# An instruction counter in the planner of a fused attention and feed-forward kernel, and a new instruction order under it

## Chip, cores, metric

One core of one Trainium2 chip. The metric is device time in microseconds (us) of that core, the median of the fast runs. A profile's span, from the first to the last instruction, is some 1.7 us shorter than the time of the same run.

## The reference, cut to what matters

Two branches read the same input (2048 x 512, bf16): A, an attention of 32 heads of 16 in 4 segments of 512 positions with a memory carried from segment to segment, and B, a gated feed-forward of width 1792. A gate mixes them.

```python
for s in range(4):                        # A
    p = softmax(qs @ ks.T * scale + mask)
    a_dot = p @ vs
    a_mem = (phi(qs) @ M) / (phi(qs) @ z + 1e-6)
    outs.append(g * a_mem + (1 - g) * a_dot)
    M = M + phi(ks).T @ vs                # the "memory burst" below
    z = z + phi(ks).sum()
a = concat(outs) @ wo
gate = x @ W_gate; up = x @ W_up          # B
b = (relu(gate) * up) @ W_down
out = sigmoid(x . gate_w) * a + (1 - ...) * b
```

## The kernel before: what the argument touches

The kernel's code contains a planner. Every piece of work is an `Op` with a planned duration on each engine that may run it. `Sched.run` simulates the engines, always taking the piece with the lowest key among those that can start soonest, and the resulting order is what is emitted. `NUDGE` holds shifts of keys that a search found. The plan fixes only the order on each engine; on the chip an instruction may still wait, as a matmul of experiment 3 did for its weights, 2.02 us.

```python
if e == "PE":
    o.ran = mode if mode in o.flex else o.mode   # tile shape: D, R, P or C
    if o.ran != mode:
        dur += SW                                # 0.094 for a change of shape
        mode = o.ran
```

TensorE's matmuls have four tile shapes here (in brackets as the profile's rows give them): D, the full array (`128*128`); R, row tiles for score blocks (`32*128`); P, for attention times V (`64*32`); C, column tiles for the memory burst (`128*32`), in which full-array work may ride along as four instructions in place of one:

```python
def mm(out_ap, lhsT, rhs, start, stop):
    if tiling[0] == "C":
        for j in range(4):
            q = slice(32 * j, 32 * j + 32)
            nc.tensor.matmul(out_ap[q], lhsT=lhsT[:, q], rhs=rhs, ..., tile_position=(0, 32 * j))   # cut
    else:
        nc.tensor.matmul(out_ap, lhsT=lhsT, rhs=rhs, start=start, stop=stop)

def mz_mm(s, g):                                 # memory burst: 64 matmuls of 34 columns, 0.56 us
    for c in range(NC):
        for t in range(4):
            for j in range(4):
                h = 8 * c + 2 * j
                nc.tensor.matmul(...)            # cut
```

Attention times V is 64 matmuls planned at 1.015 us. Each matmul has a weight load of its own (the trace of before has 1024 of each for the 16 blocks of attention times V, 192 of each for the three memory bursts), so both are bursts of 128 instructions. The program opens with warm-up matmuls that compute nothing:

```python
for _ in range(31):
    nc.tensor.matmul(g_dummy.t[:, 0:P], lhsT=ones, rhs=ones, start=True, stop=True)
```

The softmax here doesn't subtract the row's maximum and nothing guards it: scores larger than these inputs give would overflow.

## Time and profile before

| | before |
|---|---|
| time | 267.15 us (266.64 to 267.41, 6 runs) |
| span of the profiled run | 265.0 us |
| TensorE busy | 256.7 us, 97% |
| longest idle time of TensorE | 1.14 us at 34.9 us, "issue" |
| changes of tile shape on TensorE | 161 |

The profile's lines are shown in the prediction. Its key habit: TensorE's busy share doesn't say whether it is full, because the profile models the ends of matmuls. Starts are what count, and weight loads, of which the trace has 2886 where it has 2853 matmuls, number the instructions: load number n is taken as instruction 2n.

### The profile page before, as it was taken

To read this page: it belongs to the slowest core of one execution; us is meant where nothing else is said; L and a number is where in the kernel's file an instruction comes from. 1 tells how busy PE (TensorE), PEld (TensorE's weight loads), DVE (VectorE), ACT (ScalarE), POOL (GpSimd) and SP (SyncE) were. 2 spreads that over 40 slices of the span, in tenths; PEclk is the share of its full clock that TensorE was granted. 3 is DMA by queue.
4 is the path that set the end of the run, shared out by engine and by line. 5 is a ranking of instruction groups with operands and counts; after the bars stand their busy time and mean duration, and the time that the engine had idled before them with its cause. 6 is when DMAs were issued, how large, how long until landed. Compare 5 with 4: busy or idle time off the path is not lost.

```text
span 265.0 us, 7147 instructions
## 1 busy us (share of the span) xinstructions
PE 256.7 (97%) x2853; PEld 116.7 (44%) x2886; DVE 183.6 (69%) x413; ACT 193.4 (73%) x187; POOL 175.2 (66%) x436
## 2 busy tenths in 40 slices
PE   8999989999999999999999999999999999999995
PEld 7443433444444443434453444444444344344454
DVE  1488878878858675787889678786987036848352
ACT  3598978988787678989787569777878656778201
POOL 8326768886878887466599878764778746665400
PEclk9999999999999999999999999999999999999999
DMA  5998296222435010001821010000021001000002
GB/s 161 294 238 194 64 332 106 91 71 82 109 92 115 22 41 22 20 2 40 161 50 49 20 43 1 2 1 22 0 56 40 0 24 41 22 0 2 2 0 79
DMA packets 27761, 17.96 MB, mean 68 GB/s; under 512 B 14032, under 2 KB 27088, under 8 KB 27728
## 3 DMA queue, kind: packets, MB, share of 16 engines
q1 hardware_dynamic: 27136, 16.72, 25.1%
q0 software_dynamic: 176, 0.52, 0.6%
q8 instruction: 22, 0.36, 0.6%
q10 hardware_dynamic: 416, 0.26, 0.3%
q14 instruction: 11, 0.09, 0.1%
HBM read 9.84 MB, written 2.10 MB: 45 GB/s over the span
## 4 chain that ended last, share of the span: by engine, by line
PE 92%; issue 3%; ACT 2%; DMA 2%; DVE 0%; ACTq 0%
PE G L264 71%; PE S L774 9%; PE G L886 7%; PE G L262 3%; DMA wk_sb<-in_A_wk_dram 2%; PE G L306 1%; PE G L647 1%; ACT E L788 1%; ACT Vp L556 0%; PE G L823 0%; ACT QT L556 0%; ACT etq L579 0%; DVE xT L429 0%; ACT os L695 0%; PE G L421 0%
## 5 line engine op out<-in xcount | busy, mean ns | idle before, releaser
L788 ACT ACTIVATE E<-S 128x2048 bf16<-128x2048 f32 x72 | 135.1, 1876 | 35.7 <-PE S L774 30.8
L798 POOL TENSOR_SCALAR_AFFINE_SELECT E<-E 64x256 bf16<-64x256 bf16 x256 | 116.1, 454 | 61.9 <-ACT E L788 48.1
L264 PE MATMUL G<-xT,wg_sb 128*128 128x512 bf16 x200 | 53.9, 380 | 0.6 <-issue 0.3
L264 PE MATMUL G<-wd_sb,hT 128*128 128x512 bf16 (+2 forms) x239 | 53.1, 354 | 1.4 <-issue 1.1
L264 PE MATMUL G<-xT,wu_sb 128*128 128x512 bf16 x196 | 53.0, 380 | 0.2
L699 DVE TENSOR_TENSOR hT<-G,os 128x512 bf16<-128x512 f32 x56 | 38.4, 686 | 19.3 <-PE G L264 12.0
L921 DVE STREAM_TRANSPOSE T<-G 128x512 f32<-128x512 f32 x44 | 29.9, 700 | 16.0 <-PE G L886 14.3
L695 ACT ACTIVATE os<-G 128x512 bf16<-128x512 f32 x56 | 33.2, 596 | 5.6 <-PE G L264 5.2
L264 PEld LDWEIGHTS <-hT 128*128 128x128 bf16 x252 | 22.2, 98 | 24.0 <-issue 2.4
L264 PEld LDWEIGHTS <-wg_sb 128*128 128x128 bf16 x208 | 18.9, 98 | 23.2 <-issue 2.5
L264 PEld LDWEIGHTS <-wu_sb 128*128 128x128 bf16 x202 | 18.7, 98 | 23.3 <-issue 2.8
L774 PE MATMUL S<-QT,K 32*128 32x192 bf16 (+7 forms) x512 | 28.6, 287 | 0.3
L735 DVE TENSOR_SCALAR os<-G,ngcol 128x512 bf16<-128x512 f32 (+2 forms) x13 | 8.7, 669 | 19.5 <-PE G L264 19.4
L774 PEld LDWEIGHTS <-K 32*128 32x128 bf16 x512 | 8.2, 92 | 30.2 <-issue 30.1
L886 PE MATMUL G<-E,Vp 64*32 64x128 bf16 (+7 forms) x512 | 19.0, 284 | 1.1 <-issue 1.1
L886 PE MATMUL G<-E,VS 64*32 64x128 bf16 (+7 forms) x512 | 18.5, 284 | 0.0
L264 PE MATMUL G<-wo_sb,oT 128*128 128x512 bf16 (+2 forms) x71 | 16.9, 355 | 0.2 <-issue 0.2
L518 POOL COPY R<-rcol 32x4 f32<-32x4 f32 x64 | 14.2, 222 | 2.9
L264 PE MATMUL G<-xT,wk_sb 128*128 128x512 bf16 x61 | 15.8, 380 | 0.2
L886 PEld LDWEIGHTS <-Vp 64*32 64x32 bf16 x512 | 12.2, 91 | 7.3 <-issue 4.9
L941 DVE TENSOR_TENSOR O<-T,sm 128x256 bf16<-128x256 f32 x32 | 14.9, 498 | 0.2
L264 PE MATMUL G<-wv_sb,xT 128*128 128x512 bf16 x62 | 14.9, 380 | 0.1
(95 smaller groups left out, 278.7 us busy)
## 6 DMA issues: line engine op xcount, KB each, us to landing
VS<-Vp SPq DMA_DIRECT2D x8, 296.0 KB, 3.6
out_dram<-os SPq DMA_DIRECT2D x15, 128.0 KB, 1.7
xn<-in_A_x_dram SPq DMA_DIRECT2D x3, 512.0 KB, 5.0
wd_sb<-in_B_W_down_dram SPq DMA_DIRECT2D x3, 512.0 KB, 3.6
wg_sb<-in_B_W_gate_dram SPq DMA_DIRECT2D x2, 512.0 KB, 6.2
wu_sb<-in_B_W_up_dram SPq DMA_DIRECT2D x2, 512.0 KB, 6.9
wg_sb<-in_B_W_gate_dram SPq DMA_DIRECT2D x3, 256.0 KB, 6.1
wu_sb<-in_B_W_up_dram SPq DMA_DIRECT2D x3, 256.0 KB, 6.4
```

Of the source, the lines that this page charges most:

```text
L262: nc.tensor.matmul(out_ap[q], lhsT=lhsT[:, q], rhs=rhs, start=start, stop=stop, tile_position=(0, 32 * j))
L264: nc.tensor.matmul(out_ap, lhsT=lhsT, rhs=rhs, start=start, stop=stop)
L518: nc.gpsimd.tensor_copy(R[s][32 * j:32 * j + 32, k, :], rcol[32 * k:32 * k + 32, cols])
L695: nc.scalar.activation(rg.t[:], g.t[:], ACT.Relu)
L699: nc.vector.tensor_tensor(h.t[:], u.t[:], rg.t[:], ALU.mult)
L735: nc.vector.tensor_scalar(ob.t[:, cs], g.t[:, 0:W], ngcol[:, tt:tt + 1], None, ALU.mult)
L774: nc.tensor.matmul(sp.t[:, j, off:off + w], lhsT=K2[s, cc].t[rows, kb, :, :].rearrange("p r k -> p (r k)"), rhs=QT[s, cc].t[rows, L - w:L] ...
L788: nc.scalar.activation(eb_.t[:], sp.t[:], ACT.Exp, scale=SCALE)
L798: nc.gpsimd.affine_select(out=v, in_=v, compare_op=ALU.is_ge, fill=0.0, base=0, pattern=[[0, 4], [1, 64]], channel_multiplier=-1)
L886: nc.tensor.matmul(gs[r].t[32 * j:32 * j + 32, L - w:L], lhsT=v, rhs=src.t[rows, j, off:off + w], start=(kb == 0), stop=(kb == 7), tile_po ...
L921: nc.vector.transpose(T.t[:].rearrange("p b e -> p (b e)"), g.t[:])
L941: nc.vector.tensor_tensor(O.t[:, :, r, :], T.t[:, :, 0:DH], sm.t[:, r, :, None].to_broadcast([P, 16, DH]), ALU.mult)
```

## The change

The intent: if TensorE's instructions are brought to it in pieces of 256 ("lines" from here on), a burst that uses up 256 in less time than fetching takes would stop. The planner gets a counter of instructions for each operation and lets none start earlier than 4.0 us after the planned start of the operation that holds the instruction 256 before its own last one (the code takes the end of the operation ahead of that one). A new search under that rule gave 86 shifts.

```diff
+FETCH, REFILL = 256, 4.0
 NUDGE = {
-    "d130.0": 50, "q21/0": 52, ...     (cut)
+    "g2.5/0": 24, "d300.0": 88, ...    (cut: 86 entries)
 }
+        o.count = count or 2 * max(1, round(engs.get("PE", 0) / MM))
...
+                    if e == "PE":
+                        k = issued[-1] + o.count * (4 if mode == "C" and "C" in o.flex else 1) - FETCH
+                        if k > 0:
+                            t = max(t, begun[bisect.bisect_left(issued, k) - 1] + REFILL)
...
+            if e == "PE":
+                begun.append(o.end)
+                issued.append(issued[-1] + o.count * (4 if o.ran == "C" and "C" in o.flex else 1))
...
-        a = op(f"pv{s}{c}", {"PE": 1.015}, ..., mode="P", alloc=gs, ...)             (cut)
+        a = op(f"pv{s}{c}", {"PE": 1.015}, ..., mode="P", count=128, alloc=gs, ...)  (cut)
```

The counts of the other bursts (memory 128, score blocks 8 for each part, denominators 8) are set likewise.

## The prediction

> **What bounds the kernel now.** I read the page first, then TensorE's waits, then the one stretch in which TensorE waits, then the DMA view of that stretch.

> From the page, busy time of TensorE, the granted clock, and the queue that carries instructions:

> ```profile
> PE 256.7 (97%) x2853; PEld 116.7 (44%) x2886; DVE 183.6 (69%) x413; ACT 193.4 (73%) x187; POOL 175.2 (66%) x436
> ...
> PEclk9999999999999999999999999999999999999999
> ...
> q8 instruction: 22, 0.36, 0.6%
> ```

> TensorE is the bound: 97% of 265.0 us at full clock, the next engine at 73%. A matmul's end is modelled, so 97% alone doesn't prove a full engine. The starts do: inside runs of full-array matmuls they lie 0.216 us apart almost everywhere (records of single instructions, not printed here). Gaps of 0.22 us more are places where one matmul record is missing, while its weight load is there (2853 matmuls, 2886 weight loads).

> All idle time of TensorE that the profile lists, as engine and line waited for, us in total, times, longest:

> ```profile
> PE G L264 <- issue: 1.7, 11, 0.2
> PE G L886 <- issue: 1.1, 1, 1.1
> PE G L306 <- PEq L1048: 0.8, 1, 0.8
> ```

> The last row is the start of the program. The first is eleven gaps of 0.16 us each where tile shapes change and a record is missing. Only the middle row is a real stop: once, 1.1 us, for nothing that a semaphore explains. TensorE waits for no other engine in this list, so no reordering can win anything from waits for data.

> The stop in the timeline of TensorE (start us, length, instruction, count, idle before it):

> ```profile
> 31.02 0.71 PE L647 MATMUL G<-Vp,pK 128*32 128x34 bf16 x64
> 31.56 0.63 PE L262 MATMUL G<-xT,wk_sb 128*32 128x512 bf16 x8
> 32.00 0.62 PE L262 MATMUL G<-xT,wg_sb 128*32 128x512 bf16 x8
> 32.43 1.05 PE L262 MATMUL G<-xT,wu_sb 128*32 128x512 bf16 x16
> 33.41 0.40 PE L774 MATMUL S<-QT,K 32*128 32x448 bf16 x8
> 33.74 0.40 PE L886 MATMUL G<-E,Vp 64*32 64x512 bf16 x4
> ...
> 34.58 0.29 PE L886 MATMUL G<-E,Vp 64*32 64x192 bf16 x7
> 36.00 0.23 PE L886 MATMUL G<-E,Vp 64*32 64x128 bf16 x1 [1.14 <-issue]
> ```

> The burst counts 64 + 32 + 8 + 64 = 168 matmuls, each with its weight load, so 336 instructions, and it breaks off in the middle of one operation (attention times V) whose sisters elsewhere run through in 1.11 us. [...]

> The DMA view of 33.0 to 34.5 us, just before:

> ```profile
> DMA  9996999999999999998997899999989988999898
> ...
> q1 hardware_dynamic: 500, 0.50, 98.0%
> q8 instruction: 1, 0.02, 5.8%
> ```

> One packet of the instruction queue moves among transfers that fill the DMA engines. Its record: start 33.09, 1.39 us long, 16,384 bytes.

> [...]22 packets of 16,384 bytes on that queue are 22 x 256 = 5632 instructions, against 2853 + 2886 = 5739 recorded on TensorE. [...]If TensorE enters a new line at weight-load count times two = 194, 450, 706 and so on (706 placed by the stop, which comes after 698 recorded instructions; the spare ones are those that run before), then from the 4th on a packet starts between 2.6 us before and 0.8 us after the first instruction of a line runs, with one exception of 2.1 us, and it brings the line after that one. So a whole line must run while the next one is fetched. [...]

> **Timing of a fetch.** The line of the stop was entered at 31.20 and the next one's first instruction ran at 36.02: 4.82 us, of which 1.90 before the packet starts, 1.39 the packet, 1.53 after it. In the quiet part of the kernel a packet starts 0.1 to 0.8 us after the entry and takes 0.9 to 1.6 us; with the 1.53 seen above my estimate there is 0.4 + 1.2 + 1.5 = 3.1 us. The fastest 256 instructions elsewhere in the trace:

> from 31.04: 3.14 us with the stop in it; from 63.47: 3.37; from 132.42: 3.12; then 4.68 and longer. The line entered at 63.52 was used up in 3.50 us, and its packet landed 2.10 us before the next was wanted, against the 1.53 needed: no stop, 0.57 us to spare. At 132 the border between lines fell inside the burst (134.02), so neither line was used fast: 6.98 us and 9.65 us.

> **The change part by part.**
> - The counter and the waiting rule are in the planner alone. They emit no instruction. The planner keeps TensorE instruction n at least 4.0 us behind the operation that holds n - 256. Cost on the chip: 0.
> - No operation, shape, buffer or engine choice is added or removed; the sum of work is the same. Column-tiled runs count four times, which is right: the 16 rows of L262 from 32.43 are 4 matmuls.
> - Removed: the stop at 34.87 to 36.00, 1.14 us by the timeline row. TensorE is full before and after it, and the attention behind it has slack, so I count all of it: -1.14 us.
> - Added: by the rule a column-tiled run next to attention times V has to be cut or the two moved apart. There are 4 such runs (L647 or L823 with L262 behind). Cutting one may cost a change of tile shape more; the planner's own figure for a change is 0.094 us, and an R block of 8 takes 0.33 in the trace against 0.229 planned without it, so 0.1 us each: 0 to +0.4 us, I take +0.2.
> - The new order is a search of its own. It can win little: there are 72 score blocks which go in and out of their tile shape whatever the order (162 runs of one shape in all), and 15 of the 16 attention times V blocks already share a change with a neighbouring score block. I take -0.15 us for that and for start and end.
> - In the first 45 us the DMA engines are full and a fetch needed 4.82 us, more than the 4.0 allowed. If a border falls badly there, up to 0.8 us of the stop stays. One chance in five: +0.1 us on average (estimate).

> Sum: -1.14 + 0.2 - 0.15 + 0.1 = -1.0 us. From 267.19 that is 266.2 us; the median of before could hide a second short stop (at 66.8, by the 0.57 us to spare) in some executions, whose range was 266.64 to 267.39, so I put the point at 266.1.

> **Rivals.**
> 1. The stop isn't the fetch but attention waiting (for a mask of GpSimd or a buffer). Then the new order moves it by chance and the time stays at 267.2 or gets worse. [...]Against: the stop is inside the operation, after 51 of its 64 matmuls, and is put down to nothing.
> 2. The rule costs more than it saves. The planner keeps TensorE idle or takes work that it would have wanted later; score blocks come later and ScalarE, which has 30.8 us of waits for the score matmuls, starves late, where attention's chain decides the end. For it: 86 shifts, many of +50 to +100, mean a plan that was forced into place. Against: TensorE has matmuls of gate, up and down in store nearly to the end. It would give 267.5 to 269.
> 3. The search found a much better plan. TensorE's list of waits adds up to 3.6 us, 0.8 of it start and about 0.6 only missing records, so even a perfect order ends at 267.19 - 1.14 - about 1 = 265 us. A gain of 2% needs 5.3 us, more than all idle time of TensorE.
> 4. Half a fix: a border in the busy first 45 us and a stop of 0.3 to 0.8 us, so 266.5 to 267.

> **Range and chances.** The mechanism gives 266.1; executions of one kernel spread by 0.75 us here, a half-fix adds 0.8, and the best that I can argue is 265. So 265.1 to 267.3. Over 2% faster is below 261.8, for which there is no idle time: 0.01. Over 2% slower is above 272.5, for which the new order would have to starve TensorE for 5 us: 0.02.

> **What would show it.** Right: in the list of TensorE's waits the row of L886 on "issue" of 1.1 us is gone and no other row of over 0.3 us has come; still 22 packets on q8; every 256 instructions take 4 us or nearly; attention times V runs through in 1.11 us each time; PE busy time the same within 1 us; the span some 264.0. Half right: a stop on "issue" in the middle of an operation at another place, before 45 us, when the DMA engines are full. Wrong: rows in which PE waits for ACT, POOL or DVE (rival 2), or a span under 263 with fewer shape changes than 161 (rival 3), or a stop on "issue" though the 256 instructions before it took 5 us or more, which would take the fetch away as the cause.

That a line is 256 instructions was assumed there; the page by itself gives 5739 recorded instructions to 22 packets, 261 to each. That a whole line runs while the next is fetched was inferred there from the packets' starts; in experiment 1, too, a packet lies between one restart and the next, 256 instructions later (restart at 45.08, packet from 46.21 to 47.17, restart at 48.53). Against a wait for data (rival 1) there stood at that time only that the stop, 1.14 us in the middle of one operation, is put down to "issue"; the rest came with the experiments. "The starts do" rests on this: full-array matmuls of 512 columns that follow each other start 0.215 to 0.228 us apart in the traces of before and of the changed kernel, from the first matmul on weights near 9 us on and where no record is missing; never closer. "At full clock" is a granted clock of 0.999.

## The result, and the profile after

The changed kernel takes **265.65 us** (265.51 to 266.07, 6 runs) against 267.15 before (6 runs). A ratio is the mean of one kernel's fast runs over the mean of the other's of the same rounds, so it isn't quite the ratio of the medians quoted: here 0.9949, interval 0.9936 to 0.9961, within 2% and 1.4 us faster.

The list of TensorE's waits of the changed kernel (engine and line waited for: us in total, times, longest); line numbers are 11 higher than before:

```profile
PE G L275 <- issue: 1.4, 9, 0.2
PE G L317 <- PEq L1059: 0.8, 1, 0.8
```

The row of attention times V on "issue" is gone and nothing has come in its place. The span fell from 265.0 to 263.9 us. The same burst in TensorE's timeline:

```profile
36.37 0.71 PE L658 MATMUL G<-Vp,pK 128*32 128x34 bf16 x64
37.01 0.40 PE L785 MATMUL S<-QT,K 32*128 32x448 bf16 x8
37.34 2.76 PE L275 MATMUL G<-xT,wk_sb 128*128 128x512 bf16 x11
40.03 0.40 PE L785 MATMUL S<-QT,K 32*128 32x384 bf16 x8
40.36 0.40 PE L897 MATMUL G<-E,Vp 64*32 64x512 bf16 x4
...
41.47 0.39 PE L275 MATMUL G<-xT,wg_sb 128*128 128x512 bf16 x1
```

Between the memory burst and attention times V there now lie 2.7 us of full-array matmuls, where before there were 32 column-tiled ones. Two instructions take the place of eight.

Where the 1.1 us of the profiled runs come from can be added up from TensorE's starts: its last matmul ended at 261.89 us and ends at 260.80, so 1.09 earlier. In before, the line behind the stopped burst began here:

```profile
36.20 0.39 PE L264 MATMUL G<-xT,wg_sb 128*128 128x512 bf16 x1
```

So attention times V took 2.46 us with the stop (33.74 to 36.20) and takes 1.11 now (40.36 to 41.47): by starts the stop cost 1.35 us. The 1.14 of its row counts from a modelled end and is too small. From the first matmul on weights to the start of the last one it is 252.25 us before and 251.09 after; the difference of 1.16 is 1.35 less some 0.2 for two more changes of shape (161 before, 163 after). The first of these matmuls came 0.07 us later, which leaves the 1.09. A profile of the changed kernel without missing records ("after_again" below) gives the cost of one change as 0.09 to 0.11 us in all of its 163, and no other excess after the start: TensorE is full, at the 0.215 to 0.228 us from start to start given above.

### The profile page after: what moved, and what is told of

Same layout as the page of the kernel before. It is cut to its first block, busy times and chain, and to the rows that moved or that the text cites. A ratio compares the mean times of both kernels' runs of the same rounds, so it can differ in the third digit from the quotient of the medians.

```text
span 263.9 us, 7083 instructions
## 1 busy us (share of the span) xinstructions
PE 257.2 (97%) x2817; PEld 116.7 (44%) x2850; DVE 183.8 (70%) x411; ACT 194.7 (74%) x189; POOL 175.6 (67%) x436
## 4 chain that ended last, share of the span: by engine, by line
PE 97%; issue 1%; DVE 0%
PE G L275 75%; PE S L785 9%; PE G L897 7%; PE G L273 2%; PE S L456 1%; PE G L317 1%; PE G L658 1%; PE G L432 0%; PE G L834 0%; DVE os L746 0%; PE S L454 0%
## 5 line engine op out<-in xcount | busy, mean ns | idle before, releaser
L275 PE MATMUL G<-xT,wg_sb 128*128 128x512 bf16 x202 | 54.7, 380 | 0.9 <-issue 0.5
L275 PE MATMUL G<-xT,wu_sb 128*128 128x512 bf16 x205 | 54.7, 380 | 0.2
L746 DVE TENSOR_SCALAR os<-G,ngcol 128x512 bf16<-128x512 f32 (+2 forms) x10 | 6.4, 644 | 20.7 <-PE G L275 20.6
L748 ACT ACTIVATE os<-G,ngcol 128x512 bf16<-128x512 f32 x8 | 5.5, 687 | 16.4 <-PE G L275 16.4
L275 PE MATMUL G<-wv_sb,xT 128*128 128x512 bf16 x63 | 15.8, 380 | 0.1
L529 POOL COPY R<-rcol 32x4 f32<-32x4 f32 x64 | 13.3, 208 | 3.1
```

The source lines that it names most:

```text
L529: nc.gpsimd.tensor_copy(R[s][32 * j:32 * j + 32, k, :], rcol[32 * k:32 * k + 32, cols])
L746: nc.vector.tensor_scalar(ob.t[:, cs], g.t[:, 0:W], ngcol[:, tt:tt + 1], None, ALU.mult)
L748: nc.scalar.activation(ob.t[:, cs], g.t[:, 0:W], ACT.Copy, scale=ngcol[:, tt:tt + 1])
```

## Experiments

"Recorded instruction n" is counted by weight loads, from the first warm-up. The stop of before came after instruction 698, and 706 is the first of the next line after it as I had counted it in the prediction; lines are 256 long, so the line of the stop began near 450. A count read so is good to a few instructions: the trace has 14 instructions of TensorE's sequencer besides, which may take places too. The stops in other kernels bear the count out: they come after recorded instruction 698 in "before, again" and in the changed kernel with 46 fewer (both below), after 700 in experiment 1. Where the edits change the warm-up, only the line borders move against the work.

**1. The fetch by itself: the memory bursts nine times over.**

```diff
-        for c in range(NC):
+        for c in [c for _ in range(9 if s in (0, 2) else 1) for c in range(NC)]:
```

> The kernel before with the two memory bursts at 31 and 132 us (64 matmuls and 64 weight loads of 32 columns, 0.56 us) written nine times each; each repeat starts its sums anew, so the result stays right. It measures the fetch by itself: 1024 instructions more in each place, 4 lines. Fetch theory: each 256 instructions of a burst take what a fetch takes, 4.8 us with the DMA engines full and 3.1 us without, with stops on issue between; 267.2 + 4 x 4.8 + 4 x 3.1 = about 298 us, 292 if the early fetches are no slower than the late ones. Rival (no fetch limit): 16 x 0.56 = 9.0 us more, 276 us.

298.38 us (one run), results right. TensorE's timeline of the first place, and then of the second:

```profile
31.37 1.42 PE L647 MATMUL G<-Vp,pK 128*32 128x34 bf16 x155
36.25 1.19 PE L647 MATMUL G<-Vp,pK 128*32 128x34 bf16 x128 [3.46 <-issue]
41.62 1.23 PE L647 MATMUL G<-Vp,pK 128*32 128x34 bf16 x128 [4.18 <-issue]
45.08 1.23 PE L647 MATMUL G<-Vp,pK 128*32 128x34 bf16 x128 [2.22 <-issue]
48.53 0.48 PE L647 MATMUL G<-Vp,pK 128*32 128x34 bf16 x37 [2.22 <-issue]
```

```profile
153.94 1.23 PE L647 MATMUL G<-Vp,pK 128*32 128x34 bf16 x128 [2.39 <-issue]
157.94 1.23 PE L647 MATMUL G<-Vp,pK 128*32 128x34 bf16 x128 [2.77 <-issue]
161.67 1.06 PE L647 MATMUL G<-Vp,pK 128*32 128x34 bf16 x108 [2.50 <-issue]
```

**2. Moving only the borders: the warm-up.** Three kernels have the order of before and another number of instructions ahead of it.

```diff
-        for _ in range(31):
-            nc.tensor.matmul(g_dummy.t[:, 0:P], lhsT=ones, rhs=ones, start=True, stop=True)
+        for n in [64] * 54 + [P] * 4:      # 54 more; 20 more: [64] * 20 + [P] * 21;
+            nc.tensor.matmul(g_dummy.t[:, 0:n], lhsT=ones, rhs=ones[:, 0:n], ...)   # 46 fewer: 8 of 496 columns
```

> The kernel before with its 31 warm-up matmuls of 128 columns replaced by 8 of 496: the same columns, 46 TensorE instructions fewer ahead of everything else, not one other instruction moved. Fetch theory: the borders of the 256-instruction lines come 46 instructions later; worked out from the starts of the weight loads of before with the stop taken out, the line over the burst at 31 us then lasts 5.4 us against the 4.8 us that the fetch needed there: no stop, about 266.0 us, and no matmul waiting for issue over 0.3 us. Rival (attention times V stops for its data, its PSUM or its shape): the order is the same, so the stop of 1.1 us stays in the same operation, 267.1 us.

> The kernel before with 27 of its warm-up matmuls split into two of 64 columns: 54 TensorE instructions more ahead of everything else, nothing else moved. Fetch theory: the line over the burst at 31 us now lasts 3.14 us without a stop, the shortest that any border gives, so the stop grows from 1.13 to about 1.7 us and falls earlier, some 54 instructions sooner: about 267.7 us. Rival: the stop stays at 1.1 us in the same matmul, 267.1 us.

> The kernel before with 20 TensorE instructions more ahead (10 warm-up matmuls split in two). It corrects the theory that missed with 54 more: the fetch starts when TensorE's sequencer enters a line, some 36 instructions ahead of execution (estimate, from where the packets of before start), so the time it has is that of 292 instructions, not 256. From the weight-load starts of before: 3.8 us at 0 instructions more (stop 1.1, so the fetch took 4.9), 6.1 us at 54 more (no stop, as seen), 5.5 us at 46 fewer (no stop, as seen), and 3.4 us at 20 more, the least of all: a stop of about 1.5 us in attention times V, if the packet waits as long as in before; 0.3 to 0.4 us over before. Rival (a change of the warm-up by itself takes the stop away): no stop, 266.0 us.

| kernel | time, runs | ratio to before | stop in the profile |
|---|---|---|---|
| 46 fewer | 265.94 (265.44 to 266.30), 6 | 0.9964 (0.9951 to 0.9976) | none |
| 54 more | 266.07 (265.46 to 267.77), 6 | 0.9975 (0.9953 to 0.9997) | none |
| 20 more | 265.66 (265.45 to 266.71), 6 | 0.9956 (0.9940 to 0.9972) | none |

46 fewer came as expected. The other two are misses: a longer stop was forecast for both and neither has any. By starts too: from the first matmul on weights to the start of the last one the kernels with 20 and 54 more take 250.90 us, before 252.25. That speaks against a wait for data, since data and order are as before. It doesn't exclude the rival with 20 more, that a change of the warm-up by itself takes the stop away: it forecast no stop and 266.0 us, and no stop came in all three. That rival falls with experiment 3, where the stop nearly goes with the warm-up untouched, and with experiment 5, where it comes back under a changed warm-up, again after instruction 698. The two misses also kill my reckoning, which took the fetch for a fixed 4.8 or 4.9 us. The packet of 20 more started at 31.78, 0.37 us after the memory burst began; that of before 2.07 us after it. What lies between is seen in the DMA views (busy tenths in 40 slices) of the kernel with 20 more from 30.4 to 31.8 us, and of before from 31.1 to 33.1 us:

```profile
DMA  0000000000000000000000000000000000000009
...
q8 instruction: 1, 0.02, 5.7%
```

```profile
DMA  0000000000000000051727598755746659899999
...
q8 instruction: 1, 0.02, 4.4%
```

In the first nothing else moves until the fetch. In the second the DMA engines fill up from 31.95 on, and the fetch begins at the very end, at 33.09, behind that traffic. It is SyncE's issue of before:

```profile
30.90 0.38 SPq L390 DMA_DIRECT2D xn<-in_A_x_dram  x1
31.34 0.49 SPq L362 DMA_DIRECT2D wg_sb<-in_B_W_gate_dram  x1
31.87 0.52 SPq L362 DMA_DIRECT2D wu_sb<-in_B_W_up_dram  x1
```

With a border 20 instructions earlier TensorE's sequencer seems to ask for the next line before these loads fill the engines. (The trace doesn't show when it asks. That it runs ahead of execution is read from packets that start before their line's first instruction runs: 36.08 against 36.39 in the changed kernel.)

**3. Taking away what the fetch queues behind.** The loads are held until VectorE has copied the memory burst's sums; a memset of one element makes them wait. TensorE's instructions and borders are exactly those of before.

```diff
+        held = []
         for o in order:
+            if o.name in ("xn1", "wg3"):
+                held.append(o)
+                continue
             tiling[0] = o.ran
             o.emit(o.eng)
+            if o.name == "mza0":
+                nc.vector.memset(xn[1].t[0:1, 0, 0:1], 0.0)
+                for h in held:
+                    h.emit(h.eng)
```

> The kernel before with one memset more: the 0.5 MB loads of the next inputs and of the third gate piece, and with them all that SyncE issues behind them, wait until VectorE has copied the first memory burst's sums, about 1.4 us later than before (32.3 instead of 30.9 us). TensorE's instructions and their line borders are exactly those of before. Theory: the stop is a fetch queued behind these loads. With DMA engines free when TensorE enters the line at 31.1 us, the packet starts by 32.5 and not at 33.1 to 34.0, lands by 33.9, and the stop is under 0.3 us; in its place the third gate piece may come up to 1.3 us late at 39 us, a wait for that DMA, so the time is 266.0 to 267.2. Rival (the line's length alone decides): the stop stays 0.8 to 1.1 us, 267.1 or more.

267.44 us (265.35 to 268.13, 6 runs), ratio 0.9996 (0.9965 to 1.0027), 0.24 over the range I gave. SyncE and TensorE in its timeline:

```profile
31.97 0.38 SPq L390 DMA_DIRECT2D xn<-in_A_x_dram  x1
```

```profile
30.74 0.71 PE L647 MATMUL G<-Vp,pK 128*32 128x34 bf16 x64
...
34.30 0.47 PE L886 MATMUL G<-E,Vp 64*32 64x192 bf16 x8
34.55 0.25 PE L886 MATMUL G<-E,VS 64*32 64x128 bf16 x8
...
41.85 1.04 PE L264 MATMUL G<-xT,wu_sb 128*128 128x512 bf16 x4 [2.02 <-DMA wu_sb<-in_B_W_up_dram]
```

The packet started at 31.80, 1.06 us after the memory burst began and not 2.07. The stop shrank to 0.18 us, inside the row at 34.30 (0.47 us for what takes 0.29 in before). In its place TensorE waits 2.02 us for weights that now come late, so nothing is won in total. The next line, entered at 34.55 with the loads now in flight, waited 4.45 us for its packet (39.00); the four lines after it waited 0.25 to 0.79. There is one profile of this kernel, but packet, loads and stop all moved as the theory has it. The cause of the long fetch is thereby shown: not the length of the line alone, but its fetch behind these loads.

**4. Before once more, as a control.**

> The kernel before, unchanged, profiled on this chip: does its stop keep its size? The line lasts 3.7 us without a stop, a fetch 3.45 to 5.4, so the stop should be between 0 and 1.7 us and in the same matmul[...]. Rival (a wait for data): 1.1 us again or elsewhere.

267.21 us (one run). The wait list:

```profile
PE G L886 <- issue: 0.8, 1, 0.8
PE G L264 <- DMA wk_sb<-in_A_wk_dram: 0.8, 1, 0.8
```

The stop is in the same place with 0.82 us (1.04 by starts), the packet again behind the loads (33.98, issued 31.70). The second row shows the other thing that varies from run to run: the wait for the first weights near 9 us, 0.12 us in the first profile.

**5. The changed kernel on other borders.** The same edits of the warm-up.

> The changed kernel once more, on the chip of this call, as the control of the next two: 265.6 us, 0.995 of before, no matmul waiting for issue over 0.3 us. If it too waits about 1 us for a gate weight near 14 us, as it did with 54 instructions more on another chip, that wait is the chip's or the run's and not those instructions'; if it doesn't, they remain suspected.

> The changed kernel with the same 54 TensorE instructions more ahead. Fetch theory: its fastest 256 instructions take 4.35 us wherever a border falls, and a fetch needs 3.1 to 4.8: no stop, or one of under 0.5 us; 265.7 us, unchanged within 0.3. If the gain of the change were luck of the borders, a stop of about 1 us would come back: 266.7 us.

> The changed kernel with 54 instructions more, once more, on another draw of the chip. Earlier it waited 1.05 us for a gate weight at 14 us and took 266.7. If the added instructions cause that (their first instruction fetch comes at 11.5 us, among the weight loads, and not at 17.8), the wait is there again, about 1 us, and the time is 1 us over the changed kernel's. If it is the run's luck in the loads, it is gone or under 0.4 us: 265.7.

> The changed kernel with 46 TensorE instructions fewer ahead. Fetch theory: no border lets it run 256 instructions in less than 4.3 us, so no stop on issue over 0.3 us; 265.7 us within 0.4, the spread coming from the waits for first weights in the first 15 us.

| kernel | time, runs | ratio to before | in the profile |
|---|---|---|---|
| changed, again | 265.74 (265.55 to 266.27), 6 | 0.9964 (0.9949 to 0.9979) | first weights 0.33 us late, no stop |
| 54 more | 266.69 (266.42 to 266.71), 5 | 0.9989 (0.9977 to 1.0002) | gate weight at 14.4 us late by 1.05 us |
| 54 more, again | 266.78 (266.59 to 267.12), 5 | 0.9994 (0.9980 to 1.0009) | the same wait, 0.82 us, no stop |
| 46 fewer | 267.31 (266.66 to 269.43), 6 | 1.0025 (0.9997 to 1.0053) | **a stop of 1.06 us** |

46 fewer is the miss that teaches most. The stop is back in the changed order:

```profile
41.40 0.24 PE L898 MATMUL G<-E,VS 64*32 64x128 bf16 x8
41.45 0.19 PE L898 MATMUL G<-E,Vp 64*32 64x64 bf16 x2
42.70 0.20 PE L898 MATMUL G<-E,Vp 64*32 64x64 bf16 x2 [1.06 <-issue]
```

The DMA view of this kernel from 36.8 to 40.3 us, from just after the line is entered to the start of its packet:

```profile
DMA  9999999999999999999999999999999999999999
...
q1 hardware_dynamic: 1264, 1.26, 106.7%
q8 instruction: 1, 0.02, 2.0%
```

The line was entered at 36.66 and its successor was wanted at about 41.45 (the stop is 1.25 us by starts), 4.8 us later, more than the rule's 4.0. But the packet began at 40.30, 3.64 us after the entry, so the line was there only at 42.70: 6.04 us. The rule doesn't exclude the stop while 2.5 MB of loads are in the way.

That the rule makes it rarer isn't shown: of the borders tried, one in four has a stop in the old order and one in three in the new. On the same edit of the warm-up the old order is faster at 46 fewer (0.9964 of before, against 1.0025), and at 54 more the two can't be told apart (0.9975 against 0.9989 and 0.9994, with intervals that overlap).

In the changed kernel as it stands the fetch started at 36.08, 1.3 us after the loads were issued (34.78) and before they filled the engines. It landed at 37.28; with experiment 1's 1.37 more the next line could run at 38.65 (my estimate). The old spacing would have wanted it at 39.84 (my estimate too: entry at 36.39, plus the line's 4.80 us of before less the stop's 1.35). So this fetch was early enough without the spacing.

The times with 54 more are misses too: 265.7 was expected of the first. Their late gate weight came in both calls and in neither profile of the changed kernel as it is, so the added instructions are suspected. How they would delay it isn't shown: the first fetch moves from 17.8 to 11.5 us, among the weight loads, but with 46 fewer (first fetch at 20) in the kernel before the same pieces took as long, 7.5 us against 5.7. This stays open.

**6. The rule without its shifts, the shifts without the rule.**

```diff
-FETCH, REFILL = 256, 4.0
+FETCH, REFILL = 256, 0.0        # new shifts, no rule; the other kernel: rule kept, NUDGE of before
```

> The kernel before with the rule and its old shifts. From the emitted order: no 256 instructions under 3.99 us, the line at 31 us lasts 4.6 us, but 172 changes of tile shape, 11 more than before. Fetch theory and the planner's 0.094 us for a change: -1.13 + 11 x 0.094 = -0.1 us, so 267.0 us, with a stop of 0 to 0.8 us if the fetch at 31 us is a slow one. Rival (a change of shape costs nothing[...]): 266.0 us. Rival (the rule makes matmuls wait for data): rows in which TensorE waits for ScalarE, VectorE or GpSimd, over 268 us.

> The changed kernel with its 86 shifts and the waiting time of its rule set to 0. From the emitted order: 164 changes of tile shape (163 with the rule), and one line of 256 instructions that runs right through the memory burst, a score block, column-tiled matmuls and attention times V at about 36 us, 1.9 us by the planner's own durations. Fetch theory, with 3.45 to 5.4 us from line to line as the burst run measured: a stop of 1.5 to 3.4 us there, 267.2 to 269.1 us. Rival (the search, not the rule, made the gain): no stop over 0.5 us, 265.7 us.

Old shifts with the rule: 268.05 us (267.48 to 268.41, 6 runs), ratio 1.0043 (1.0028 to 1.0058). No stop on issue, though this fetch also started behind the loads (packet at 33.01, loads issued at 31.05) and ended just in time: landed 34.73, plus experiment 1's 1.37 is 36.10, and the next line's first instruction ran at 36.13. Here the rule by itself is seen to work, for it had stretched that line to 4.8 us. Its price: 172 changes of shape, 11 more than before at 0.10 us, and

```profile
PE G L275 <- DVE T L932: 0.8, 3, 0.4
```

waits of TensorE for VectorE. I had expected 267.0; the missing 1 us is in these: by starts TensorE has 1.3 us of excess beside the changes of shape, 0.52 of it at 38.6 us and 0.49 at 254.3.

New shifts without the rule: 271.20 us (270.99 to 272.17, 5 runs), ratio 1.0170 (1.0152 to 1.0188). The expected stop did not come: the burst ran through in 2.07 us, its packet having started at 36.11, 0.70 us before the line's first instruction (36.81), well ahead of the loads' traffic, and its landing at 37.44 plus 1.37 is 38.81, when the next line was due at 38.71: just in time, with a line of only 1.90 us. The loss is elsewhere:

```profile
PE S L785 <- ACT E L799: 3.0, 2, 2.0
```

Two score blocks near 80 us wait for ScalarE: the order is just a poor one. Shifts belong to the plan under which they were searched, so this kernel says nothing on the rule's worth, and "the search made the gain" isn't shown either.

**All lines together.** The times, read from single records of the traces: first instruction of the line (450), start and landing of its successor's packet, issue of the `xn` load, first instruction of the next line; the stop is as its row lists it.

| kernel | loads issued | line entered | packet | landed | next line ran | stop |
|---|---|---|---|---|---|---|
| before | 30.90 | 31.20 | 33.09 | 34.49 | 36.00 | 1.14 |
| before, again | 31.70 | 32.00 | 33.98 | 35.20 | 36.49 | 0.82 |
| before, late loads | 31.97 | 30.92 | 31.80 | 33.01 | 34.55 | 0.18 |
| before, 20 more | 31.29 | 31.53 | 31.78 | 33.06 | 34.86 | 0 |
| before, 54 more | 31.60 | 31.73 | 32.10 | 33.45 | 34.87 | 0 |
| before, 46 fewer | 31.68 | 32.23 | 34.87 | 35.86 | 37.51 | 0 |
| old shifts, rule | 31.05 | 31.35 | 33.01 | 34.73 | 36.13 | 0 |
| changed | 34.78 | 36.39 | 36.08 | 37.28 | 41.09 | 0 |
| changed, 46 fewer | 34.91 | 36.66 | 40.30 | 41.43 | 42.70 | 1.06 |

The four profiles not listed (changed, again; 54 more, twice; new shifts without the rule) have no stop here, and their packets started at most 0.90 us after the loads' issue. Packets either start at most 1.3 us after the loads' issue or 2.0 to 5.4 us after it; all stops over 0.2 us are in the second group, and there the lines that last 4.8 us or longer without the stop escaped in two cases of three.

No version beats the changed kernel. The old order with 20 warm-up instructions more reaches the same time, 0.9956 against 0.9949 and 0.9964 of before. Without its stop the old order is if anything the shorter one, 250.90 us from the first matmul on weights to the start of the last against 251.09: the two changes of shape.

## Why the prediction was right, point by point

- **The stop removed, -1.14 us: right that it goes and that it is the whole gain, but the term is too small.** By starts the stop cost 1.35 us in the first profile of before and 1.04 in the second; the prediction took its row, which counts from a modelled end. TensorE's end moved by 1.09. Over all runs the gain is larger, 1.36 us (0.9949 of 267.1). That the unprofiled rest is the start's varying wait for the first weights (0.12 and 0.79 us in two profiles of before) is likely, but not shown.
- **The cause, a fetch of 256 instructions: right, shown by the 128 matmuls from stop to stop.** Rival 1, a wait for data, fell when the stop came back after instruction 698 in another order and under another warm-up.
- **The cure, 4.0 us of spacing: not shown to be what helped here; this part is luck.** In the changed kernel the fetch got ahead of the loads, and then even a line of 1.90 us ran without a stop (new shifts without the rule). Spacing by itself is seen to work in one profile, old shifts with the rule, and to fail in another, 46 fewer.
- **Shape changes, +0.2 us: right in size.** Two more, 0.10 each.
- **A better order, -0.15 us: not found.** TensorE has no other excess in either order. It didn't matter for the sum.
- **Rule by itself costly (rival 2): true of the rule with old shifts**, 268.05 us, within the 267.5 to 269 that I gave for it. The search under the rule is what brought this price back to +0.2.
- **Two lines misread.** "3.14 us with the stop in it" is without it: the 256 instructions from 31.04 end at 34.18, before the stop at 34.87. And all eleven gaps of the row of 1.7 us are missing records, for "before, again", which has none missing, doesn't have the row; so rival 3's "about 1" us of further room wasn't there.
- **Queue 8: half read.** The 22 packets of 16,384 bytes are on q8, but the same page lists `q14 instruction: 11`, packets of 8,192 bytes. Whose they are isn't shown.
- **"In the first 45 us the DMA engines are full": the wrong account.** The DMA view of before from 0 to 46 us has 0 or 1 tenth from 27.60 to 32.20 and 9 tenths from there to 41.40, after one particular set of loads was issued (from 30.90 on). Whether the fetch got ahead of them decided, as experiments 2 and 3 show. My 3.1 us for a quiet fetch was too small (3.45 at the least); that I counted from execution and not from when the sequencer asks may be the reason, but isn't shown.
- **"Half a fix" (rival 4) did not happen in the changed kernel, but is one warm-up edit away from it** (46 fewer, 267.31 us), and there it is larger than the 0.8 us allowed for: 1.25 by starts.

## What to carry to other kernels

When TensorE stops in the middle of one operation for "issue", count instructions back by weight loads and look in the DMA view for a packet of the instruction queue shortly before: a burst of small tiled matmuls may have outrun its own code, as that of experiment 1 did after every 128 of them. Here spacing the burst, letting the border fall elsewhere and keeping bulk loads from being issued just before it each removed the stop or nearly so, but the first and the last won no time; 46 instructions fewer in the warm-up brought it back (1.06 us), so check other borders before crediting an order. A rule added to a planner needs its own search: here shifts found under one plan lost 1 us or more under another. And measure a stop from start to start, against a sister that runs through: its row showed 0.2 us too little.
